# Attention and expert layers in one kernel: the first expert's first rows gathered after five batches instead of six, and the sixth batch's scatters spaced like those of the first five

## The chip, the cores and the metric

The kernel runs on one core of one Trainium2 chip. The metric is the device time of one execution in microseconds (us); less is better. The core has five engines that run side by side, each with its own queue of instructions, worked off in order: TensorE (PE, matmuls; PEld are its weight loads), VectorE (DVE), ScalarE (ACT), GpSimd (POOL) and SyncE (SP, which here only issues transfers). Transfers are issued from SP, ACT and POOL and run on 16 shared DMA engines.

## The reference

Causal attention with a decay, and then a layer of eight experts of which each token uses one:

```python
# q, k, v: 8 batches x 8 heads x 576 x 64; f: 8 x 8 x 576
cum = np.cumsum(np.log(np.clip(f, 0.0001, 1.0)), axis=-1)
scores = scale * q @ k.T + cum[..., :, None] - cum[..., None, :]     # above the diagonal: -1e9
attn = exp(scores - max) ; attn /= attn.sum(-1) + 1e-09
x = (attn @ v) as 4608 tokens x 512
logits = x @ w_gate ; e_idx = argmax(logits) ; gate_w = softmax(logits)[e_idx]
eom = sigmoid(x @ w_output_gate)
for e in range(8):                      # every token belongs to one expert
    h = maximum(x[e_idx == e] @ w1[e], 0)          # 512 -> 1024
    out[e_idx == e] = gate_w * eom[:, e] * (h @ w2[e])   # 1024 -> 512
```

With the inputs of the reference's default seed expert 0 gets 582 of the 4608 tokens: 434 of the first 3456 (six batches), and 360 of the first 2816, which is what five routed batches hold here (why not 2880 is told below).

## The kernel before, in words

**Two phases.** Attention and routing are one loop of steps (`attention`, L738), written out by hand: `now[0]` is the step, 192 of them do scores, and every piece of work is placed by an offset of the table `OFF` and, inside a step, by `OFF["order"]`. Each engine gets its instructions in just this order. Six steps make one pair of heads (u = 0 to 31), 24 steps one batch. Then come the experts, expert 0 first.

**Attention in a step.** PE makes a bank of scores (`sc`, L273), ACT takes the exponential (`p`, L381), POOL subtracts the upper half of each number from it (`plo`, L383; from step 181 on every second one is DVE's), and PE multiplies `p` and `plo` with V (`av`, L455 to L457 and L466 to L468). For the first head of a pair, the third bank's `plo` is made in step 6u+4 and read by PE in step 6u+6. Before a pair's scores SP writes the row maxima into the tile `Eq` (`max_put`, L361 and L363, at step 6u-5), and the scores of step 6u-1 read them. DVE normalizes (L488 to L495), POOL also splits V (`Vs`, L145).

**From attention to the experts.** When half of a batch's heads (u of 16) is done, `feats` casts the rows to pairs of 16-bit numbers (ACT L527, L145), five or four transposing transfers on SP make `xT` for the router (`feats_turn`, L534), and `feats_out` writes the rows to `xbuf` in DRAM (L541). A batch has 4 tiles of 128 tokens and 64 more. The last 64 of an even batch share a tile with those of the odd batch after it: they are written (two L546, one for each batch) and routed with the odd batch. So the first five batches (0 to 4) hold 4 x 576 + 512 = 2816 routed tokens, and the last 64 rows of batch 4 are written when batch 5 is, its second half at step 163.

**Routing.** `route` (L558) makes logits on PE (`lg`, L566, L567), ranks the tokens of the batch within each expert on DVE and PE, and then POOL scatters each tile's tokens into the table `tbl` (L650, one transfer to a tile), whose first rows are those of expert 0. `apart` says how many POOL operations lie between two scatters; the first scatter comes 13 steps after the route begins. For batch 5 neither held before: it scattered as soon as its ranks were there, with one operation between. `lg` and `rk` of the router, the small transposes and `hold` take turns in one PSUM bank (`tag="ms"`).

**The early rows.** The first three tiles (384 rows) of expert 0 are fixed before attention ends. `hold_early` (L548) counts expert 0's rows so far; where there are fewer than 384, it moves later rows of expert 0 behind row 384 and leaves the slots between empty. `early_gather` (L720) waits for the last scatter, reads the table's first 384 entries (`ids`, L701), gathers the rows on POOL into `xg` (L705, three transfers) and transposes them on SP (L711, three). Each gather reads `xbuf[0:known]`, where `known` is `EARLY_B * S`, and so it waits for every write into that part of `xbuf`.

**After attention.** PE does expert 0's up products on the three early tiles (`hp`, L934). Behind the sixth of eight groups of them stand the logits of batch 7, the last. Its scatters, then `ids` (L701), gathers and transposes lead to the rest of expert 0 and to expert 1. SP's queue holds the transposes for the logits of batch 7 behind all that stands before them. `CAP` is 640: an expert with more rows (expert 0's empty slots counted) would need another pass at the end.

Of the kernel before, what the change touches and what calls it, by code (L numbers as in the profile page):

```python
# [21 lines left out]
B, H, S, D = 8, 8, 576, 64  # L22
# [21 lines left out]
NSLOT = P  # L44
WSC = 64.0

EARLY_B = 6
ET = 3
EARLY = ET * P

# [2 lines left out]
OFF = {  # L53
    "crow": -12, "clear": -16, "clearstep": 1, "prefill": -11, "fetch": -23, "spread": -21, "max": -15, "pair": -8,
    "mturn": -7, "rows": -6, "put": -5, "rscore": 2, "rexp": 3, "av": 5, "fetch_v": (-19, -25, -21), "v": ((-2, -9, -16), (1, -7, -15)), "apart": 2, "scatter": 13,
    "feats0": 19, "feats1": 20, "fturn": 21, "fturnstep": 2, "fout": 31, "route": 45, "rank": 6, "w1r": 10, "w1": 48, "w1step": 2, "w2": 4,
    "hold": 188, "gather": 180, "ids": 5, "landed": 1, "gturn": 2, "route_last": 200, "nsum": 8, "nrec": 9, "nx": 9, "nrest": 10,
    "mv": ["xr", "v0", "v1"], "begin": -18, "wg": -4, "spread/1": -11,
    "steps": [0, 0, 0, 0, 0, 1, 8, 1], "dve": [181, 183, 185, 187, 189, 191],
    "order": "reduce put feats1 v0 scores nrec max pair rows spread feats0 fetch "  # L60
             "fetch_v fturn extra tick mturn tick v1 nx rexp av rscore maxrest route fout tick exps nsum tick nrest",
# [11 lines left out]
def _attn_moe(ctx, tc, qk, vm, f, wg, w1, w2, out):  # L73
# [67 lines left out]
    pooled = [0]  # L141
# [39 lines left out]
    apart = cp.tile([1, 1], F32, name="apart")  # L181
# [325 lines left out]
    last = 3 * HU * NU  # L507
# [48 lines left out]
    now = [0]  # L556

    def route(b, t0=None):  # L558
# [79 lines left out]
        for t in range(nt):  # L638
            at, n = now[0], pooled[0]
            yield  # L640

            while t0 is not None and b < EARLY_B - 1 and now[0] < t0 + OFF["scatter"]:
                yield

            while t0 is not None and now[0] < last and (now[0] == at or pooled[0] < n + (OFF["apart"] if t and b < EARLY_B - 1 else 1)):
                yield
            if b == B - 1 and t:

                nc.gpsimd.memset(apart, 0.0)
            ins = nc.gpsimd.indirect_dma_start(  # L650
                out=tbl, out_offset=bass.IndirectOffsetOnAxis(ap=pi[:, t:t + 1], axis=0),
                in_=rec[:, b, t], in_offset=None)

            for other in scatters:
                tc.declare_no_dep(ins.ins, other.ins, reason="distinct rows")
            scatters.append(ins)
# [47 lines left out]
    def gather_rows(x, t, known=NT):  # L704
        nc.gpsimd.indirect_dma_start(  # L705
            out=xg[:, t], out_offset=None, in_=xbuf[0:known],
            in_offset=bass.IndirectOffsetOnAxis(ap=x[0][:, t, 0:1], axis=0),
            bounds_check=known - 1, oob_is_err=False)
# [11 lines left out]
    def early_gather():  # L720
        while len(routed) < EARLY_B:
            yield

        at = now[0]
        while now[0] < at + OFF["landed"]:
            yield
        x = st["early"] = gather_ids(ar, tbl[0:EARLY], ET)
        at = now[0]
        for t in range(ET):
            while now[0] < at + OFF["ids"] + t:  # L730
                yield
            gather_rows(x, t, EARLY_B * S)
        for t in range(ET):
            while now[0] < at + OFF["ids"] + OFF["gturn"] + t:
                yield
            gather_turn(x, t)

    def attention():  # L738
# [12 lines left out]
        for s in range(OFF["begin"], last + OFF["nrest"] + 1):  # L751
# [80 lines left out]
            def extras():  # L832
                for f, fc in extra.get(s, ()):
                    f(fc)
                if s == OFF["hold"]:
                    assert routed == list(range(EARLY_B))
                    hold_early()
# [251 lines left out]
```

## Time and profile before

| | us |
|---|---|
| three runs | 832.22, 838.12, 838.7 |
| median | 838.12 |
| profiled execution, whole | 837.48 |
| its span, first to last instruction | 835.8 |
| attention, to the last `rk` matmul | about 387 |

The profile is one execution. A row of the timeline gives start and duration in us, engine, line, operation, output and input, how many were merged, and in brackets how long the engine had been idle before and what ended it. A row of the list of waits gives the total, how often, and the longest. A row of the windows gives the window and its length, the busy time and count of PE, PEld, DVE, ACT and POOL, then the granted TensorE clock (1.00 is 2.4 GHz, 0.50 is 1.2 GHz), the DMA engines' share and GB/s.

### The profile page before, as it was taken

To read this page: it belongs to the slowest core of one execution; us is meant where nothing else is said; L and a number is where in the kernel's file an instruction comes from. 1 tells how busy PE (TensorE), PEld (TensorE's weight loads), DVE (VectorE), ACT (ScalarE), POOL (GpSimd) and SP (SyncE) were. 2 spreads that over 40 slices of the span, in tenths; PEclk is the share of its full clock that TensorE was granted. 3 is DMA by queue.
4 is the path that set the end of the run, shared out by engine and by line. 5 is a ranking of instruction groups with operands and counts; after the bars stand their busy time and mean duration, and the time that the engine had idled before them with its cause. 6 is when DMAs were issued, how large, how long until landed. Compare 5 with 4: busy or idle time off the path is not lost. (4 is left out here: it accounts for less than half of the span.)

```text
span 835.8 us, 21243 instructions
## 1 busy us (share of the span) xinstructions
PE 765.8 (92%) x8814; PEld 499.7 (60%) x8814; DVE 348.6 (42%) x770; ACT 344.8 (41%) x767; POOL 475.1 (57%) x504
## 2 busy tenths in 40 slices
PE   1699999899999999977939999999999999999997
PEld 0377776667776676755516565656656566565653
DVE  4456676675868575735412511203112031120310
ACT  6055565465655564534302423415234153331420
POOL 9088778688887788865252523625437254361301
PEclk9999999999999999979978999999999999999999
DMA  3333758866697668327749554655645556444201
GB/s 102 127 122 79 183 146 178 167 151 143 151 186 154 105 156 117 96 65 126 128 105 280 194 97 144 180 128 170 161 131 160 131 166 167 124 140 101 73 14 43
DMA packets 132920, 112.61 MB, mean 135 GB/s; under 512 B 96024, under 2 KB 105426, under 8 KB 132820
## 3 DMA queue, kind: packets, MB, share of 16 engines
q1 hardware_dynamic: 121092, 75.19, 40.7%
q0 software_dynamic: 7552, 18.92, 7.4%
q10 hardware_dynamic: 4176, 17.11, 7.2%
q8 instruction: 70, 1.15, 0.6%
q14 instruction: 30, 0.25, 0.1%
HBM read 72.79 MB, written 20.48 MB: 112 GB/s over the span
## 5 line engine op out<-in xcount | busy, mean ns | idle before, releaser
L383 POOL TENSOR_TENSOR plo<-p 128x512 f16<-128x512 f32 x186 | 197.9, 1079 | 71.3 <-ACT p L381 69.4
L934 PE MATMUL hp<-xT,w1h 128*128 128x384 f16 (+1 forms) x1024 | 197.2, 303 | 19.8 <-DMA xT<-xg 18.2
L299 DVE TENSOR_REDUCE nR<-mx 128x2 f32<-128x1024 f32 (+4 forms) x160 | 126.6, 808 | 90.0 <-PE mx L273 77.8
L381 ACT ACTIVATE p<-sc 128x512 f32<-128x512 f32 x192 | 112.9, 595 | 80.0 <-PE sc L273 70.0
L934 PEld LDWEIGHTS <-w1h 128*128 128x128 f16 x1024 | 101.1, 99 | 66.2 <-DMA xT<-xg 14.4
L273 PE MATMUL sc<-qk 64*128 64x512 f32 (+4 forms) x640 | 137.2, 488 | 0.0
L934 PE MATMUL hp<-xT,w1l 128*128 128x384 f16 (+1 forms) x512 | 129.9, 303 | 0.0
L967 POOL DMA_INDIRECT out_dram<-ys,ids x40 | 41.8, 1046 | 151.5 <-ACT ys L966 103.3
L944 DVE SCALAR_TENSOR_TENSOR hl<-hp,hh 128x256 f16<-128x256 f32 (+1 forms) x128 | 60.5, 491 | 155.6 <-ACT hh L943 143.8
L963 PE MATMUL y<-w2l,hh 128*128 128x512 bf16 x320 | 120.5, 379 | 0.0
L962 PE MATMUL y<-w2h,hh 128*128 128x512 f16 x320 | 120.3, 379 | 0.0
L964 PE MATMUL y<-w2h,hl 128*128 128x512 f16 x320 | 119.3, 379 | 0.0
L273 PEld LDWEIGHTS <-pick 64*128 64x128 bf16 (+1 forms) x1152 | 64.0, 99 | 47.6 <-issue 25.1
L896 DVE TENSOR_TENSOR w2l<-w2r,w2h 128x512 bf16<-128x512 f32 x28 | 26.9, 961 | 148.7 <-ACT w2h L895 148.7
L966 ACT ACTIVATE ys<-y,ids 128x512 f32<-128x512 f32 x40 | 27.5, 687 | 134.6 <-PE y L964 95.2
L455 PE MATMUL av<-Vs,p 128*128 128x65 f16 x640 | 70.6, 195 | 10.0 <-ACT xr L502 6.4
L273 PE MATMUL mx<-qk 64*128 64x256 bf16 (+5 forms) x384 | 64.8, 312 | 14.8 <-DVE nR L299 8.8
L671 POOL TENSOR_TENSOR w1l<-w1r,w1h 128x512 bf16<-128x512 f32 x48 | 54.8, 1160 | 38.3 <-ACT w1h L670 38.2
L943 ACT ACTIVATE hh<-hp 128x256 f16<-128x256 f32 (+1 forms) x128 | 50.6, 433 | 58.6 <-PE hp L934 52.1
L670 ACT CAST w1h<-w1r 128x512 f16<-128x512 f32 x64 | 39.1, 617 | 85.6 <-issue 46.3
L457 PE MATMUL av<-Vs,plo 128*128 128x65 f16 x640 | 69.8, 193 | 4.8 <-POOL plo L383 4.6
L456 PE MATMUL av<-Vs,p 128*128 128x64 bf16 x640 | 70.1, 196 | 0.0
(156 smaller groups left out, 1424.6 us busy)
## 6 DMA issues: line engine op xcount, KB each, us to landing
qk<-in_qk_dram ACTq DMA_DIRECT2D x29, 576.0 KB
w1r<-in_w_dram SPq DMA_DIRECT2D x64, 256.0 KB
w2r<-in_w_dram SPq DMA_DIRECT2D x64, 256.0 KB
v<-in_vm_dram SPq DMA_DIRECT2D x16, 576.0 KB
xbuf<-x SPq DMA_DIRECT2D x16, 512.0 KB
qk<-in_qk_dram SPq DMA_DIRECT2D x3, 576.0 KB
xT<-x SPq DMA_TRANSPOSE x72
Eq<-mts SPq DMA_DIRECT2D x64, 0.1 KB
```

What stands on the lines that cost most here:

```text
L273: nc.tensor.matmul(dst(i), w(i), x(i), start=start, stop=stop)
L299: nc.vector.tensor_reduce(o, x, axis=AX.X, op=ALU.max, negate=True)
L381: nc.scalar.activation(out=f32, in_=src, func=AF.Exp, scale=0.125)
L383: eng.tensor_tensor(lo, f32, upper(f32), op=ALU.subtract)
L455: nc.tensor.matmul(dst, ph, vv[:, 0:W], start=kc == 0, stop=False)
L456: nc.tensor.matmul(dst[:, 0:D], ph, vv[:, W:].bitcast(BF16), start=False, stop=False)
L457: nc.tensor.matmul(dst, pl, vv[:, 0:W], start=False, stop=kc == qc)
L934: nc.tensor.matmul(m[:, 0:(t1 - t0) * P], w[:, k], xT[:, t0:t1, k // 2, j, k % 2], start=k == 0 and i == 0, stop=k == ND - 1 and i == 2)
L944: nc.vector.scalar_tensor_tensor(hl[:, fc, sl], m, 0.0, hh[:, fc, sl], op0=ALU.max, op1=ALU.subtract)
L962: nc.tensor.matmul(y, hh[:, fc, sl], wh, start=fc == 0, stop=False)
L963: nc.tensor.matmul(y, hh[:, fc, sl], wl, start=False, stop=False)
L964: nc.tensor.matmul(y, hl[:, fc, sl], wh, start=False, stop=fc == NF - 1)
```

## The change

The early rows come from five batches, the offsets of `hold` and `gather` move from steps 188 and 180 to 167 and 156, and the spacing rule of the scatters holds for batches 0 to 5, where it held for 0 to 4.

```diff
-EARLY_B = 6
+EARLY_B = 5
...
-    "hold": 188, "gather": 180, "ids": 5, "landed": 1, "gturn": 2, "route_last": 200, "nsum": 8, "nrec": 9, "nx": 9, "nrest": 10,
+    "hold": 167, "gather": 156, "ids": 5, "landed": 1, "gturn": 2, "route_last": 200, "nsum": 8, "nrec": 9, "nx": 9, "nrest": 10,
...
-            while t0 is not None and b < EARLY_B - 1 and now[0] < t0 + OFF["scatter"]:
+            while t0 is not None and b < B - 2 and now[0] < t0 + OFF["scatter"]:
                 yield

-            while t0 is not None and now[0] < last and (now[0] == at or pooled[0] < n + (OFF["apart"] if t and b < EARLY_B - 1 else 1)):
+            while t0 is not None and now[0] < last and (now[0] == at or pooled[0] < n + (OFF["apart"] if t and b < B - 2 else 1)):
                 yield
```

**POOL, the early gathers.** Before, they stood at steps 186 to 188, close to the end of attention:

```order
L383 TENSOR_TENSOR plo<-p_8219 128x512
L383 TENSOR_TENSOR plo<-p_8179 128x512
L705 DMA xg<-xbuf,ids 128x1024
L383 TENSOR_TENSOR plo<-p_8360 128x512
L705 DMA xg<-xbuf,ids 128x1024 x2
L397 TENSOR_TENSOR prl_97<-prf_96 128x128
```

Now they stand at steps 165 to 167, among the splits of V:

```order
L383 TENSOR_TENSOR plo<-p_7402 128x512
L705 DMA xg<-xbuf,ids 128x1024
L397 TENSOR_TENSOR prl_97<-prf_96 128x128
L383 TENSOR_TENSOR plo<-p_7456 128x512
L145 TENSOR_TENSOR Vs_93<-v_6851,Vs_93 128x9x64
L705 DMA xg<-xbuf,ids 128x1024
L383 TENSOR_TENSOR plo<-p_7402 128x512
L705 DMA xg<-xbuf,ids 128x1024
L383 TENSOR_TENSOR plo<-p_7456 128x512
```

The `plo` ahead of the third gather is that of step 166. Three gathers have moved ahead of some thirty POOL operations, and two of them now stand ahead of this `plo`. Batch 5's scatters, which stood one operation apart at steps 174 to 178, now begin at step 178 and stand two or three apart, the last at step 189.

**SP around the early gathers, as it is now** (`Eq` is the maxima's tile, `Ek` the decay's, `xT<-xg` the early rows' transposes, the other `xT` the router's):

```order
L701 DMA ids<-tbl 128x3x2
L534 DMA_TRANSPOSE xT_6937<-x_6938 128x4x128
L361 DMA Eq_87<-mts 2x4x128
L363 DMA Eq_87<-mts 1x16x4 x2
L541 DMA xbuf<-x_6938 128x4x512
L546 DMA xbuf<-x_6938 64x512 x2
L256 DMA Ek_80<-crow 6x576
L534 DMA_TRANSPOSE xT_7432<-x_7433 128x4x128 x2
L711 DMA_TRANSPOSE xT<-xg 128x8x128 x2
L361 DMA Eq_88<-mts 2x4x128
L363 DMA Eq_88<-mts 1x16x4 x2
```

`ids` and the three `xT<-xg` are what is new here. The first L546 writes the last 64 rows of batch 4, which the gathers read; it is issued at step 163, and the first gather stands at step 165.

**SP at the end of attention**, before:

```order
L711 DMA_TRANSPOSE xT<-xg 128x8x128
L534 DMA_TRANSPOSE xT_8378<-x_8379 128x4x128
L711 DMA_TRANSPOSE xT<-xg 128x8x128 x2
L534 DMA_TRANSPOSE xT_8378<-x_8379 128x4x128 x4
L541 DMA xbuf<-x_8379 128x4x512
L546 DMA xbuf<-x_8379 64x512 x2
L534 DMA_TRANSPOSE xT_8711<-x_8712 128x4x128 x5
```

And now:

```order
L534 DMA_TRANSPOSE xT_8391<-x_8392 128x4x128 x5
L541 DMA xbuf<-x_8392 128x4x512
L546 DMA xbuf<-x_8392 64x512 x2
L534 DMA_TRANSPOSE xT_8711<-x_8712 128x4x128 x5
```

The early rows' transposes no longer stand among those of batch 7, on which its logits wait.

## Rows read from the trace of the kernel before

**Rows 1.** The page: busy us of each engine, share of the span, instructions.

```profile
PE 765.8 (92%) x8814; PEld 499.7 (60%) x8814; DVE 348.6 (42%) x770; ACT 344.8 (41%) x767; POOL 475.1 (57%) x504
```

**Rows 2.** The list of waits, 340 to 470 us: total, times, longest.

```profile
PE hp L934 <- DMA xT<-xg: 18.2, 2, 14.1
...
PE av L457 <- POOL plo L383: 4.6, 1, 4.6
```

**Rows 3.** The timeline of PE: matmuls before which it had been idle.

```profile
363.95 0.23 PE L457 MATMUL av<-Vs,plo 128*128 128x65 f16 x1 [4.61 <-POOL plo L383]
379.54 0.33 PE L273 MATMUL rs<-qk 64*64 64x64 f32 x4 [0.65 <-DVE x L145]
391.42 0.80 PE L934 MATMUL hp<-xT,w1h 128*128 128x384 f16 x2 [4.11 <-DMA xT<-xg]
439.96 0.61 PE L934 MATMUL hp<-xT,w1h 128*128 128x256 f16 x2 [14.13 <-DMA xT<-xg]
```

**Rows 4.** Windows in which the granted clock went back up.

```profile
372.00:374.00 2.00, 2.00 (x44) 1.91 (x40) 0.00 (x0) 1.50 (x3) 0.90 (x1) 0.58 0.04 8
394.00:396.00 2.00, 2.00 (x13) 1.16 (x12) 0.52 (x1) 0.49 (x1) 0.46 (x1) 0.96 0.83 187
445.00:450.00 5.00, 5.00 (x46) 4.41 (x44) 1.52 (x4) 1.54 (x4) 0.95 (x1) 0.96 1.10 211
```

**Rows 5.** The timeline of POOL at steps 165 to 167.

```profile
334.77 0.40 POOL L397 TENSOR_TENSOR prl<-prf 128x128 f16<-128x128 f32 x1
...
336.13 1.25 POOL L145 TENSOR_TENSOR Vs<-v,Vs 128x576 bf16<-128x576 f32 x1
337.34 2.04 POOL L383 TENSOR_TENSOR plo<-p 128x512 f16<-128x512 f32 x2
```

**Rows 6.** The timeline of POOL: scatters, the late `plo`, and a gather.

```profile
324.20 0.99 POOL L650 DMA_INDIRECT tbl<-rec,pi  x1 [0.17 <-issue]
...
361.56 1.25 POOL L650 DMA_INDIRECT tbl<-rec,pi  x1 [0.17 <-issue]
362.84 3.03 POOL L383 TENSOR_TENSOR plo<-p 128x512 f16<-128x512 f32 x3
...
374.30 1.36 POOL L705 DMA_INDIRECT xg<-xbuf,ids  x1 [0.15 <-issue]
```

**Rows 7.** The timeline of PE: a wait for maxima, step 167's `av`, step 173's scores.

```profile
328.18 0.39 PE L273 MATMUL sc<-Eq,Ek 64*128 64x512 f16 x2 [1.46 <-DMA Eq<-mts]
...
340.05 0.20 PE L455 MATMUL av<-Vs,p 128*128 128x65 f16 x1
...
347.90 1.13 PE L273 MATMUL sc<-qk 64*128 64x512 f32 x4
```

**Rows 8.** The timeline of SP's queue at steps 157 to 169.

```profile
319.22 0.61 SPq L361 DMA_DIRECT2D Eq<-mts  x1
...
335.73 1.54 SPq L546 DMA_DIRECT2D xbuf<-x  x2
...
341.76 0.60 SPq L361 DMA_DIRECT2D Eq<-mts  x1
```

**Rows 9.** The timeline of SP's queue: `ids` and the first early transpose.

```profile
367.24 0.40 SPq L701 DMA_DIRECT2D ids<-tbl  x1
...
378.12 1.24 SPq L711 DMA_TRANSPOSE xT<-xg  x1
```

**Rows 10.** The window in which the transfers of step 163 end.

```profile
338.00:339.00 1.00, 1.00 (x8) 0.43 (x8) 0.93 (x3) 0.00 (x0) 1.00 (x2) 1.00 0.34 96
```

**Rows 11.** The timeline of SP's queue after attention.

```profile
385.15 3.44 SPq L711 DMA_TRANSPOSE xT<-xg  x2
...
396.23 8.43 SPq L534 DMA_TRANSPOSE xT<-x  x5
```

**Rows 12.** The last cast of batch 7 on DVE, and its logits on PE.

```profile
391.00 0.42 DVE L145 TENSOR_TENSOR x<-xr,x 128x256 f16<-128x256 f32 x1
...
405.49 0.19 PE L566 MATMUL lg<-wgs,xT 128*128 128x32 f16 x1 [0.16 <-DMA xT<-x]
```

## The prediction

> **What bounds the kernel now.** I read the page first, then the waits around the change, then the timeline of each engine there. TensorE is busy 92% of the span [rows 1], so a gain can only come from the few places where it stands still or runs at half clock. In the list of waits from 340 to 470 us two names matter: `plo` of POOL, 4.6 us once, and the early and later rows' transposes, 18.2 us in two waits [rows 2]. The timeline gives the places [rows 3]: PE stands 4.61 us until 363.95 (so from 359.34) for a `plo` that POOL makes behind batch 5's crowded scatters [rows 6]; 4.11 us until 391.42, between attention and the first `hp`, for the early rows; and 14.13 us until 439.96 for the rest of the rows, after a long chain that starts with batch 7's logits.
>
> After each of these waits the granted clock is 0.50 for a while. It returns in the windows of [rows 4]; a window at 0.58 of 2 us was full for 0.32 us, so after the first wait it returned at 373.7, 9.7 us after PE had started again. By the same reading it took 2.7 us after the second wait and 5.4 us after the third. Half clock costs half of that time where PE sets the pace: 4.9, 1.4 and 2.7 us.
>
> **The change part by part.**
>
> *Batch 5's scatters.* They were five in a row with one operation between, and the last `plo` behind them came at 362.84 to 363.9 [rows 6]. Now only one stands ahead of that `plo` (step 178). What this wait cost is 4.61 + 4.9 = 9.5 us. That goes, if POOL comes to step 178 in time. The other four scatters lie where the gathers were, about 1.4 us each against 1.5 us each; nothing there changes.
>
> *The gathers.* Three operations of 0.15 + 1.36 = 1.5 us [rows 6] move ahead to steps 165 to 167, where POOL starts its `prl` at 334.77 [rows 5]. Their place isn't empty, and the first one has a new wait. It reads `xbuf` up to row 2880, and the last 64 rows of that are written by the first L546, which SP issues at 335.73 [rows 8], after POOL has come to the gather. Those transfers end in the window from 338 to 339, a third of the way in by its DMA share [rows 10]: 338.4. SP is also a little later than before, since `ids` now stands ahead and waits for batch 4's last scatter. That one ends at 325.2, and a last scatter that ended at 362.8 let `ids` go at 367.24, 4.4 us later [rows 6, 9]: `ids` goes at 329.6 and costs the queue between nothing and 2 us; I take 0.7. So the first gather starts at about 339.1, and POOL, which works in order, does nothing from 334.8 until then. Then come gather 1.5, `prl` 0.4, `plo` 1.0, V's split 1.25, gather 1.5 and step 166's `plo` 1.0 [rows 5, 6]: 345.8. PE reads it right after the nine matmuls of step 167 that begin at 340.05 [rows 7], at about 340.35. **A new idle time of 5.4 us takes the place of the old one.** It is as long as those after which the clock fell; half clock then costs 1.4 to 4.9 us, and between the three rows I take the middle one, 2.7, since the nearest in place (4.9) had POOL behind as well. In sum 8.1 us (6.8 to 10.3) instead of 9.5: a gain of 1.4 (2.7 to -0.8).
>
> The Trainium skill's page "TensorE: Matmul & The Clock Gate", section "HAM oscillation — how this bites in real kernels", speaks against the change here: a long wait inside a stream of matmuls lets the gate fall, and the work after it starts slow, each time anew. By that the moved idle pays for the clock again, as in the sum; were the clock to stay, the sum would be 830 (POOL would then set the pace at step 178). All three waits of over 4 us in this trace agree with the page.
>
> *Does the old wait come back?* From 345.8 to step 178's `plo` POOL has one gather, twelve `plo`, three splits of V, two `prl`, one scatter and a small product: 1.5 + 12.2 + 3.75 + 0.8 + 1.4 + 0.3 = 20 us, so 365.8. PE, 8.1 us late, wants it at 367.5, and at 366.1 in the mildest case. So no second stall, by little.
>
> *`hold`.* Its matmul and three small DVE operations are the same. They share a PSUM bank with the small transposes, and the matmul behind waited 0.65 us [rows 3]; at step 167 that falls into the new idle time: a gain of 0.65.
>
> *`ids` and the transposes on SP.* The three L711 leave the end of attention. There two of them held SP's queue for 3.44 us [rows 11], ahead of nine of batch 7's ten transposes. Batch 7's last cast ended at 391.4 [rows 12], yet its last five transposes began at 396.23 [rows 11], and the logits waited for them at 405.49 [rows 12]. So the queue, not the data, was late, and the logits come 3.4 us earlier after attention's end (0 if the transfers themselves set the pace, 5.5 if all of what PE gains counted). From the logits to 439.96 the chain is the same work, so the end moves by that much.
>
> *The wait at 391.42* goes whole, with its half clock: 4.11 + 1.4 = 5.5 us of PE time. Counted at 3.4 only, already above: PE comes earlier to batch 7's logits, and now waits there about 2 us for SP. The 14.13 us wait stays.
>
> *The data.* With 360 early rows, 24 slots stay empty; 582 + 24 = 606 is under 640, so no pass is added. The gathers move the same three tiles.
>
> **The sum.** 1.4 + 0.65 + 3.4 = 5.4 us off the profiled execution's 837.5: **832 us**. That execution is 0.6 us under the median of 838.1. This case's own range is 829 to 836: the half clock gives 1.3 down and 2.2 up, the queue at the end 2 us each way.
>
> The Trainium skill's "DMA: Bandwidth & Descriptors", section "Anatomy of one DMA — SWDGE (gpsimd) path", gives a transfer issued by POOL about 2.0 us in all before its bytes count. By it `ids` would go over 3 us sooner, the 0.7 us would be nothing, and the sum 831.4. The trace shows 5.7 us from the scatter's start to `ids` [rows 6, 9], and that decides.
>
> **The rivals.**
>
> *The gathers hold nothing up.* If the 64 rows have landed when POOL gets there, step 166's `plo` ends at 341.5 and PE waits 1.1 us, step 178's at 361.4 and PE waits 0.9 more: 2.0 instead of 9.5 us. With 3.4 at the end that is 10.9 off: **826.6**. For it: POOL may come later than in this trace. Against it: 335.73 is after 334.77 without any delay, and SP only gets more to do.
>
> *The transposes on SP hold up the maxima: slower than before.* Two L711 stand ahead of the put for the scores of step 173. The second waits for the second gather, which ends at 344.8; a gather that ended at 375.66 let its transpose go at 378.12 [rows 6, 9], 2.5 us later, or 4.4 as after the scatter. So the put, at 341.76 before [rows 8], goes at 348.5 to 350.5. The scores stood at 347.90 [rows 7] and are 8.1 us late, 356.0. This decides from about 7 us of landing on: a put begun at 319.22 kept PE until 328.18 [rows 7, 8], 9 us, with the queues full. Then PE waits another 2.5 us or so and the clock falls again (1.4 to 4.9): up to 7.4 us more, **839 to 840**. Twice in a row, for the next pair as well, would be 847. Against it: 328.18 is the only such wait I found late in attention.
>
> *The end doesn't move.* If batch 7's transposes run at the pace of the DMA engines (the last five took 8.43 us [rows 11]), nothing is won there, and it is **835.5**. Against it: 4.8 us between the last cast and the first of the five.
>
> **How the numbers follow.** Forecast 0.52, gathers free 0.18, SP slower 0.12, end unmoved 0.18. The range that leaves out no more than 2 in 10 is 825 to 840: it takes in the forecast's own range, the third rival and most of the first two. Within 1% (8.4 us, about what a measurement of this kernel can tell from no change, as its three runs span 6.5) means 829.7 to 846.5. Faster: most of the first rival and the forecast's low end, 0.27. Slower: the second rival doubled, 0.06. Same: 0.67.
>
> **What would show it.** Right: POOL stands some 4 us before its first gather; PE stands about 5 us near 340 on `plo`, with clock 0.50 after it; none near 360; `hp` follows `rk` without a gap; the last five `xT` transposes begin within 2 us of the last cast; the 14 us wait is still there. Wrong: a wait on `Eq` near 356, a late `plo` near 366, or logits that come no sooner after the last cast. Above 840 or under 825 a step that I have not seen is at work.

## The result, and the profile after

| | before | changed |
|---|---|---|
| median of 11 runs each, us | 837.36 | 842.31 |
| lowest to highest | 832.22 to 841.7 | 838.72 to 846.0 |
| profiled execution, its span | 837.48, 835.8 | 845.94, 844.2 |

The ratio is 1.0059, 95% interval 1.0034 to 1.0084: slower by 5 us, where 5.4 us less were forecast. A repeat on another chip, where the kernel before took 829.56, gave 1.0039 (1.0019 to 1.0059). The ratios leave out executions over 1.5% above the fastest of their kernel, which the medians keep: one of six in e9 and five of twelve in e10, whose medians alone give 0.993 and 0.991, and one each in e12 and e15. The profile shown in this section is 3.6 us above the median of its kernel.

The list of waits of PE, 300 to 470 us, answers to [rows 2]: total, times, longest.

```profile
PE hp L934 <- DMA xT<-xg: 15.5, 1, 15.5
PE lg L566 <- DMA xT<-x: 10.1, 3, 5.2
PE av L457 <- POOL plo L383: 4.4, 1, 4.4
```

The `hp` wait for the early rows is gone. A `plo` wait is there, but at a new place. A wait that was not in the sum has come in: the router's logits (`lg`) wait for their transposes. PE's timeline gives the places, as in [rows 3].

```profile
342.94 0.21 PE L566 MATMUL lg<-wgs,xT 128*128 128x32 f16 x1 [4.41 <-DMA xT<-x]
...
353.45 0.23 PE L457 MATMUL av<-Vs,plo 128*128 128x65 f16 x1 [4.41 <-POOL plo L383]
...
393.87 0.48 PE L934 MATMUL hp<-xT,w1h 128*128 128x384 f16 x2
...
411.85 0.21 PE L566 MATMUL lg<-wgs,xT 128*128 128x32 f16 x1 [5.16 <-DMA xT<-x]
...
450.12 0.61 PE L934 MATMUL hp<-xT,w1h 128*128 128x256 f16 x2 [15.51 <-DMA xT<-xg]
```

Two waits of 4.41 us stand in the middle of attention: batch 5's logits, and ten us later the `plo` behind the gathers. None is near 360, and `hp` follows without a gap. The windows (the granted clock is the third number from the end) show a granted clock of 0.62 to 0.70 around and behind both.

```profile
340.00:345.00 5.00, 2.06 (x23) 1.46 (x25) 0.92 (x4) 0.00 (x0) 0.00 (x0) 0.67 0.64 101
345.00:350.00 5.00, 3.79 (x45) 2.06 (x41) 2.12 (x3) 1.66 (x3) 2.54 (x4) 0.65 0.57 138
350.00:355.00 5.00, 1.55 (x15) 1.24 (x17) 3.67 (x11) 0.31 (x1) 4.62 (x5) 0.70 0.56 143
355.00:360.00 5.00, 5.00 (x68) 3.48 (x66) 0.93 (x3) 1.97 (x7) 5.00 (x6) 0.62 0.46 102
```

SP's queue shows where it starts, first its list of waits and then its timeline, as in [rows 8, 9].

```profile
SPq L701 <- DMA tbl<-rec,pi: 8.5, 1, 8.5
```

```profile
337.96 0.40 SPq L701 DMA_DIRECT2D ids<-tbl  x1
338.83 1.24 SPq L534 DMA_TRANSPOSE xT<-x  x1
...
343.61 1.47 SPq L546 DMA_DIRECT2D xbuf<-x  x2
```

`ids` stood 8.5 us at the head of the queue. Behind it stood the last transpose for batch 5's logits, which is PE's first wait, and the 64-row write, on which the first gather waits. POOL's timeline, as in [rows 5, 6], has the other end.

```profile
325.85 0.99 POOL L650 DMA_INDIRECT tbl<-rec,pi  x1 [0.17 <-issue]
...
347.44 1.06 POOL L705 DMA_INDIRECT xg<-xbuf,ids  x1 [12.40 <-DMA Ek<-crow]
...
352.35 1.05 POOL L383 TENSOR_TENSOR plo<-p 128x512 f16<-128x512 f32 x1
```

Batch 4's last scatter starts at 325.85, and what reads it goes 12.1 us later. POOL then stands 12.40 us ahead of the first gather. (The row names the transfer that came last by the profile; by the program the gather waits for `ids` and the 64 rows.)

**Where the 8.4 us between the two profiles are.** Three points cut the span: the start of batch 4's last scatter (324.20 and 325.85), the last `rk` of attention (batch 6's), the last `lg` of batch 7, and the late `hp` at 439.96 and 450.12. The first stretch is cut once more: PE's idle time (gaps of over 0.15 us), and what half clock took, which is (1 - granted clock) times PE's busy time, summed over windows of 2 us.

| profile | scatter to last rk | idle | clock | rest | rk to last lg | lg to late hp |
|---|---|---|---|---|---|---|
| before | 62.9 | 7.4 | 4.8 | 50.7 | 18.9 | 33.9 |
| changed | 68.0 | 10.2 | 5.2 | 52.5 | 19.1 | 37.2 |

1.65 us of the 8.4 lie ahead of the change, 5.1 in the first stretch, 0.2 and 3.2 in the other two, and behind the late `hp` 1.8 come back.

### The profile page after: what moved, and what is told of

Read it like the earlier page. It is cut to its first block, busy times and chain, and to the rows that moved or that the text cites. A ratio compares the mean times of both kernels' runs of the same rounds, so it can differ in the third digit from the quotient of the medians.

```text
span 844.2 us, 21239 instructions
## 1 busy us (share of the span) xinstructions
PE 768.9 (91%) x8814; PEld 500.7 (59%) x8814; DVE 349.4 (41%) x770; ACT 344.7 (41%) x767; POOL 473.9 (56%) x504
## 5 line engine op out<-in xcount | busy, mean ns | idle before, releaser
L896 DVE TENSOR_TENSOR w2l<-w2r,w2h 128x512 bf16<-128x512 f32 x28 | 25.1, 896 | 149.7 <-ACT w2h L895 149.7
L273 PE MATMUL mx<-qk 64*128 64x256 bf16 (+5 forms) x384 | 65.3, 315 | 13.9 <-DVE nR L299 8.3
```

Of the source, the lines that this page charges most:

```text
L273: nc.tensor.matmul(dst(i), w(i), x(i), start=start, stop=stop)
```

## The experiments

Theory 1 when they began: `ids` waits for batch 4's last scatter at the head of SP's queue, and makes the logits and the 64-row write late; PE pays for both, and for the clock. Theory 2: only the gather's wait for the 64 rows. Theory 3: the gathers' own load on POOL. The experiments ran in four sessions on chips on which the kernel before took 828.01 (e1 to e4), 829.56 (e5 to e8), 836.89 (e9 to e12) and 829.16 us (e13 to e16), so each is read as a ratio to the kernel before on its chip.

**e1, ids late.**

```diff
-    "hold": 167, "gather": 156, "ids": 5, "landed": 1, "gturn": 2,
+    "hold": 167, "gather": 156, "ids": 5, "landed": 7, "gturn": 2,
```

> One number changed against the changed kernel: ids is read seven steps after batch 4's last scatter instead of one, so at step 166, behind batch 5's last logits transpose and the 64-row write on SP's queue; the gathers move with it to steps 171 to 173, their transposes to 173 to 175. Theory 1 (ids, waiting for the scatter's 11 us landing at the head of SP's queue, makes both the logits of batch 5 and the 64 rows late): the lg wait near 343 (4.4 us) and the plo wait near 353 (4.4 us) both go, SP waits under 1 us on ids, the first gather runs without an idle POOL ahead of it, and the time falls by 9 to 14 us against the changed kernel: 829 to 833. Theory 2 (only the gather's wait for the 64 rows): the plo wait goes and the lg wait stays: 5 to 7 us less, 835 to 837. Theory 3 (the load of three gathers on POOL itself, 4.5 us in a busy stretch): a plo wait of 3 to 5 us turns up near 365 to 375 instead, and the time is as in the changed kernel, 839 to 843.

829.87 us, ratio 1.0020 (0.9997 to 1.0042). The `plo` wait fell to 0.2 us, batch 5's logits did not wait, and POOL was not idle ahead of its gather, as theory 1 had it. But by the two ratios only about half of the slowdown went (the changed kernel has 1.0039 in e5, and the two intervals overlap), not the 9 to 14 us expected. PE had new waits, for the maxima of DVE (`nR`):

```profile
356.27 0.40 PE L273 MATMUL mx<-qk 64*128 64x256 bf16 x2 [2.92 <-DVE nR L299]
```

**e2, known.**

```diff
-            gather_rows(x, t, EARLY_B * S)
+            gather_rows(x, t, EARLY_B * S - EARLY_B % 2 * SR)
```

> One bound changed against the changed kernel: the early gathers read xbuf only up to row 2816, which holds every row that five routed batches can name, so they no longer wait for the 64-row write of step 163. ids stays at step 160 and still waits for the scatter. Theory 1: the lg wait (4.4 us, with its half clock) stays as it is, SP still stands about 8 us at ids; the first gather goes at about 340.5 instead of 347.4, as soon as ids has landed, and the plo wait near 353 goes or shrinks under 1.5 us: 4 to 7 us less than the changed kernel, 835 to 838. Theory 2 (only the 64 rows): both waits go, 829 to 832. Theory 3 (POOL's load): the plo wait stays at 3 us or more, 840 to 843.

827.31 us, ratio 0.9992 (0.9972 to 1.0012). The first gather went 12.0 us behind the scatter (318.13 to 330.13), not 21.6, and PE waited 1.07 us for `plo`. The interval lies wholly under that of the changed kernel (1.0019 to 1.0059), so the wait for the 64 rows is most of its loss. All the same it is no faster than before, and here the trace shows why: PE, DVE and POOL, a timeline of each.

```profile
351.61 0.29 PE L273 MATMUL mx<-qk 64*128 64x256 bf16 x2 [3.30 <-DVE nR L299]
```

```profile
343.79 5.70 DVE L620 TENSOR_TENSOR tmp<-tmp,oh 128x40 f32<-128x40 f32 x1
...
350.27 1.28 DVE L299 TENSOR_REDUCE nR<-mx 128x2 f32<-128x768 f32 x2
```

```profile
342.50 1.24 POOL L145 TENSOR_TENSOR Vs<-v,Vs 128x576 bf16<-128x576 f32 x1
343.70 0.39 POOL L397 TENSOR_TENSOR prl<-prf 128x128 f16<-128x128 f32 x1
344.06 2.03 POOL L383 TENSOR_TENSOR plo<-p 128x512 f16<-128x512 f32 x2
346.06 0.19 POOL L627 TENSOR_TENSOR sc<-sc 128x5 f32<-128x5 f32 x1
346.21 1.22 POOL L145 TENSOR_TENSOR Vs<-v,Vs 128x576 bf16<-128x576 f32 x1
347.40 2.03 POOL L383 TENSOR_TENSOR plo<-p 128x512 f16<-128x512 f32 x2
```

L620 works on 128x40 numbers and took 0.20 us in the kernel before (at 348.01). Here it stands 5.70 us, from 343.79 to 349.49, and POOL's unbroken row of operations ends at 349.43. The reduction that PE waits for stands behind it in DVE's queue. In e1 L637 took 2.83 us in place of 0.16, until 355.01, and POOL's row ended at 355.00. I call this theory 1b: the moved gathers take POOL's pauses, and a DVE operation with two operands in SBUF stands until POOL pauses. It is theory 3 in another form: the load is paid on DVE, not on `plo`. Two limits belong to it. Not every such operation stood until the end of the row: in e1 L594 stood 1.10 us until 339.37, when one of POOL's operations ended (339.31) and the next followed at once. And in the changed kernel's own two profiles L620, the cast L629 and L637 took 0.16 to 0.20 us; only `hold`'s L554 stood there, 2.98 us in the first profile, while PE waited for `plo` anyway.

The Trainium skill's page "SBUF — State Buffer", section "Who interferes with whom", has it that VectorE and GpSimd share a port pair, which one of them holds for a whole instruction, and that a VectorE instruction with two SBUF inputs, or a copy or cast in a fast mode, competes for it. The traces agree; that the loser can stand over a row of POOL instructions, seven in the trace of e2, is what they add.

**e3, batch 5 as tight as before.**

```diff
-            while t0 is not None and b < B - 2 and now[0] < t0 + OFF["scatter"]:
+            while t0 is not None and b < B - 3 and now[0] < t0 + OFF["scatter"]:
...
-... (OFF["apart"] if t and b < B - 2 else 1)):
+... (OFF["apart"] if t and b < B - 3 else 1)):
```

> The changed kernel with the old spacing for batch 5 alone: its scatters stand one POOL operation apart again and begin as soon as its ranks are there; the early rows still come from five batches at steps 165 to 167. All theories have the two waits near 343 and 353 stay as in the changed kernel. If the spacing was worth the 9.5 us that I counted (4.6 us of waiting near 360 and 4.9 us of half clock), this is 7 to 10 us slower than the changed kernel: 849 to 852. If PE, being late by 10 us or more from the two new waits, has already given POOL the time that it lacked, no wait shows near 360 to 375 and it is within 2 us of the changed kernel.

836.87 us, ratio 1.0112 (1.0094 to 1.0131), and the changed kernel has 1.0039 in e5: the spacing is worth about 0.7%, 6 us, a little under the 7 to 10 expected. PE's timeline has both waits, the one of the gathers and the old one, the latter as long as in [rows 3]:

```profile
342.63 0.23 PE L457 MATMUL av<-Vs,plo 128*128 128x65 f16 x1 [7.85 <-POOL plo L383]
...
368.57 0.20 PE L457 MATMUL av<-Vs,plo 128*128 128x65 f16 x1 [4.61 <-POOL plo L383]
```

**e4, the read alone in the kernel before.**

```diff
+            if s == 160:
+                nc.sync.dma_start(ar.tile([P, CT, 2], I32, name="ids")[:, 0:ET],
+                                  tbl[0:EARLY].rearrange("(t p) c -> p t c", p=P))
```

> The kernel before with one transfer more: at step 160 SP also reads the table's first 384 entries, into a buffer that nothing uses; gathers, hold and spacing are those of the kernel before. It is the read of ids alone at its new place. Theory 1: SP stands 7 to 10 us at this read until about 338, batch 5's last logits transpose behind it is late, and PE waits 4 to 5 us for lg near 343; PE and POOL have then a new relation, so the wait for plo near 360 (4.6 us) may shrink: the time is 836 to 844, and the profile decides. Theory 2 and 3 (the read itself is harmless): the read waits under 2 us, no lg wait over 1 us, time within 1.5 us of the kernel before.

828.84 us, ratio 1.0013 (0.9990 to 1.0036), no `lg` wait, and 2.3 us of waiting at the read, for a transpose. It went at 326.92, 8.5 us behind its scatter (318.40). Against theory 1: the read alone does PE no harm in this trace. (In the first profile, where it went 12.1 us behind, it did, through the logits.)

**e5, the changed kernel once more,** without an edit.

> The changed kernel itself, not edited, once more: the chip of the first four experiments ran the kernel before in 828.0 us, the chip of the first comparison in 837.4, so the changed kernel needs a time beside theirs. Theory 1: ids waits 7 to 12 us for batch 4's last scatter at the head of SP's queue, the 64-row write goes behind it, PE loses 8 us or more before 360 in one or two waits (lg, plo) and 4 to 6 us to the half clock after them, and logits of batch 7 come no sooner after the end of attention: 1.004 to 1.008 of the kernel before. If the slowdown belongs to that one chip: 0.994 to 1.001.

831.55 us, ratio 1.0039 (1.0019 to 1.0059). Its profile is the fastest of its runs, 825.91, so it shows a mild case. It has one wait in place of two. PE, SP and POOL:

```profile
342.50 0.24 PE L457 MATMUL av<-Vs,plo 128*128 128x65 f16 x1 [7.31 <-POOL plo L383]
```

```profile
325.67 0.40 SPq L701 DMA_DIRECT2D ids<-tbl  x1
...
331.56 1.99 SPq L546 DMA_DIRECT2D xbuf<-x  x2
```

```profile
336.49 1.06 POOL L705 DMA_INDIRECT xg<-xbuf,ids  x1 [7.67 <-DMA xbuf<-x]
```

`ids` goes 6.9 us behind the scatter (318.77), the logits do not wait, and yet the gather comes at 336.49, 17.7 us behind the scatter, since the write is issued 12.8 us behind it and the gather follows another 4.9 later. Of the changed kernel's two profiles the `lg` wait belongs to the first alone, the wait for the 64 rows to both. Even in this mild case the loss in attention is there: idle 9.5 and clock 3.1 us, 64.4 in the table's first stretch.

**e6, known and ids late.** The edits of e1 and e2 together.

```diff
-    "landed": 1,
+    "landed": 7,
...
-            gather_rows(x, t, EARLY_B * S)
+            gather_rows(x, t, EARLY_B * S - EARLY_B % 2 * SR)
```

> Two edits against the changed kernel: the gathers read xbuf only up to row 2816 (no wait for the 64-row write), and ids is read seven steps after batch 4's last scatter (gathers at steps 171 to 173). Theory 1: each edit alone takes the two waits away, and together they give nothing more than one: within 2 us of the kernel with ids late alone; the wait for nR of DVE near 356 (2.9 us there) stays, since it comes from the ranks of batch 5 on DVE and not from the gathers. Theory 2: as theory 1. Theory 3 (POOL's load): also the same. If the two add up, it is 3 us or more below either.

832.02 us, ratio 1.0039 (1.0017 to 1.0061). The gathers now hold up nothing (`plo` 0.38 us), and L637 stands 2.84 us, with 3.77 us of waiting for `nR` behind it. Nothing is won over the changed kernel (1.0039 too): one wait has taken the other's place.

**e7, the last write behind the transposes.**

```diff
-                fturn=turns, fout=lambda: each("fout", NQ - 1, 12, feats_out),
+                fturn=turns, fout=lambda: each("fout", NQ - 2, 12, feats_out),
...
+        feats_out(NQ - 2)
```

> One thing moved against the changed kernel: the last feats_out that stands between the two groups of five transposes for batch 7's logits (one L541 of 512 rows and two L546 of 64 rows, written to xbuf) goes behind both groups. If these writes hold up the last transposes, the logits of batch 7 end 4 to 5 us sooner after attention (14 to 15 us behind the last rk instead of 19), the wait of 15.5 us for the later rows starts as much earlier, and the time is 3 to 5 us under the changed kernel on the same chip. If the transposes run at the DMA engines' own pace, or the tables and gathers behind them then wait for the writes instead, nothing moves: within 1.5 us.

827.31 us, ratio 1.0000 (0.9974 to 1.0027), 4 us under the changed kernel. From the last `rk` to the last `lg` it is 13.8 us, 15.6 in e5: the write between the two groups of five transposes had held up the second. The two profiles are equally long (825.99 and 825.91), so of the 4 us they show only these 1.7.

**e8, all three:** the edits of e1, e2 and e7, whose added lines are these.

```diff
-    "landed": 1,
+    "landed": 7,
...
+            gather_rows(x, t, EARLY_B * S - EARLY_B % 2 * SR)
...
+        feats_out(NQ - 2)
```

> The three edits together: gathers read up to row 2816, ids seven steps after the scatter, and the last feats_out behind batch 7's last transposes. Theory 1 has no wait of over 3 us in attention, hp behind rk without a gap, and at the end what the last feats_out alone brings: 8 to 12 us under the changed kernel, 3 to 7 us under the kernel before (0.992 to 0.996). If the writes at the end are not what is late: as the kernel with the first two edits.

829.07 us, ratio 0.9994 (0.9966 to 1.0023). L637 stood 2.84 us again, and in a profile 3.2 us above the median idle and clock in attention came to 8.3 and 6.5. Theory 1 alone had missed this.

**e9, known and ranks in PSUM.** The edit of e2, and:

```diff
-        nc.vector.tensor_tensor(tmp, rkv, eoff[:, 0:nt], op=ALU.add)
+        nc.vector.tensor_tensor(rkv, rkv, eoff[:, 0:nt], op=ALU.add)
...
-        nc.vector.tensor_tensor(tmp, tmp, oh, op=ALU.mult)
+        nc.vector.tensor_tensor(tmp, rkv, oh, op=ALU.mult)
...
-        so = ar.tile([P, E], BF16, name="so")
+        so = rk[:, NTB * E:NTB * E + E]
```

> The kernel whose gathers read up to row 2816 (known), and in the router three operands moved from SBUF to PSUM: the ranks' sum is written back into the bank of rk, and the small counts go there too, so that the two DVE operations of batch 5's ranks (L620, L637) read one operand from SBUF instead of two. With known alone, L620 stood 5.70 us from 343.79 to 349.49, until the last of POOL's unbroken run of operations had ended (349.43), and PE waited 3.30 us for nR behind it and lost 3.1 us to half clock. Theory 1b (a DVE operation with two operands in SBUF stands while POOL works without a pause, and the moved gathers have taken POOL's pauses): L620 and L637 take 0.2 us each wherever POOL is, the wait for nR near 34 us after batch 4's last scatter goes, and the time is 2 to 6 us under known alone, 0.992 to 0.997 of the kernel before. Rival (DVE is late for another reason, or the long row is an artefact of the trace): the wait for nR stays at 2.5 us or more, ratio 0.998 to 1.002.

831.35 us, ratio 0.9889 (0.9833 to 0.9945). In the profile L620 takes 0.20 us, and the next operation with its operands in SBUF stands in its place, a cast; DVE and POOL:

```profile
349.14 0.20 DVE L620 TENSOR_TENSOR tmp<-rk,oh 128x40 f32<-128x40 f32 x1
...
349.64 5.18 DVE L629 CAST pi<-sc 128x5 int32<-128x5 f32 x1
...
355.05 0.16 DVE L637 TENSOR_TENSOR runs<-runs,rk 128x8 bf16<-128x8 bf16 x1
```

```profile
352.76 2.03 POOL L383 TENSOR_TENSOR plo<-p 128x512 f16<-128x512 f32 x2
```

It stands until 354.82; POOL's row ends at 354.79. The wait for `nR` went, one of 4.28 us for L637 took its place (the bank of `rk` is now held until then). This profile (834.85) is 3.5 us above the median and shows no gain over e2's in the first stretch (65.3 against 63.1 us); the gain of e9 rests on its times alone.

**e10, the same with the last write moved,** the edits of e9 and e7:

```diff
+        nc.vector.tensor_tensor(tmp, rkv, oh, op=ALU.mult)
...
+        feats_out(NQ - 2)
```

> As the one before, and the last feats_out behind batch 7's last transposes. Theory 1b and the end together: logits of batch 7 end 13.8 to 14.1 us behind the last rk, no wait of over 2 us in the last 60 us of attention: 0.990 to 0.995 of the kernel before, under both kernels. If something else becomes late in attention again, 0.997 or more.

829.43 us, ratio 0.9859 (0.9818 to 0.9900). Here POOL pauses between 349.43 and 349.85, and the cast, at 349.69, takes 0.17 us. The last `lg` comes 15.1 us behind `rk`, later than the 13.8 to 14.1 expected.

**e11, gathers behind the ranks,** with the edit of e7 and

```diff
-    "landed": 1,
+    "landed": 10,
```

> The changed kernel with ids ten steps behind batch 4's last scatter, so that the gathers stand at steps 174 to 176, behind batch 5's ranks and ahead of its first scatter (step 178), and with the last feats_out moved as before. Theory 1b: POOL keeps its pauses while batch 5's ranks are made, L620 and L637 take 0.2 us, no wait for nR near 34 us after the scatter; instead POOL has three gathers and the first scatter in five steps, 4.5 us more than it has room for, so plo is late by 1 to 4 us near step 178: 0.995 to 1.000. If the wait for nR is there as before (2.5 us or more), theory 1b falls.

835.36 us, ratio 0.9987 (0.9955 to 1.0018). L620, L629 and L637 did not stand, and `plo` was 1.85 us late near step 178, both as expected of theory 1b. DVE's casts of the rows and one `plo` of its own stood (1.95 to 2.93 us); in the kernel before one of each did too (1.98 and 2.19).

**e12, the last write moved in the kernel before.**

```diff
-                fturn=turns, fout=lambda: each("fout", NQ - 1, 12, feats_out),
+                fturn=turns, fout=lambda: each("fout", NQ - 2, 12, feats_out),
...
+        feats_out(NQ - 2)
```

> The kernel before, with the last feats_out behind batch 7's last transposes and nothing else. In the kernel before SP reaches those transposes 3 us later, because of the early rows' transposes ahead of them, so the writes are hidden less or more: if the logits of batch 7 end 1.5 to 2 us sooner after the last rk than 18.6 to 18.9, as they do in the changed kernel, the time is 1 to 2 us under the kernel before (0.997 to 0.999); if SP's queue alone sets them there, 1.000.

834.73 us, ratio 0.9966 (0.9929 to 1.0003): not told apart from no change, and the last `lg` came 18.3 us behind `rk`, hardly sooner.

**e13, the changed kernel with ranks in PSUM,** now the positions too: the edits of e9 without that of e2, and

```diff
+        pos = rk[:, NTB * E + E:NTB * E + E + nt]
         nc.vector.tensor_reduce(pos, tmp, axis=AX.X, op=ALU.add)
```

> The changed kernel with the router's ranks made through PSUM: the sum of L616 stays in the bank of rk, and the positions (L623) and counts (L635) go there too, so that L620, the cast L629 and L637 have at most one operand in SBUF or none of the size that stood. Gathers, ids and writes are as in the changed kernel. Theory 1 (ids on SP's queue, then the gather's wait for the 64 rows): POOL stands 7 to 12 us ahead of its first gather as before, PE waits 7 us or more in one or two places near 15 to 28 us behind batch 4's last scatter, so PE is late and POOL has pauses when batch 5's ranks come: nothing to win, 1.002 to 1.007 of the kernel before, as the changed kernel. If the moved gathers cost by the lock alone, it is 0.990 to 0.997.

826.24 us, ratio 0.9969 (0.9948 to 0.9990). PE waits 8.31 us for the `plo` behind the gathers, as theory 1 said, but the time is under its range of 1.002 to 1.007, since ranks in PSUM gain in the kernel before as well (e14). The gain over the changed kernel (0.7%) is about what they gain there.

**e14, the kernel before with ranks in PSUM,** the edit of e13:

```diff
+        pos = rk[:, NTB * E + E:NTB * E + E + nt]
```

> The kernel before with the same ranks through PSUM and nothing else. In its trace L620, L629 and L637 of batch 5 took 0.16 to 0.20 us each, so theory 1b gives it nothing there: 0.997 to 1.002. If the ranks of other batches stood behind POOL too, or PSUM is better in itself, it is under 0.994, and the gain of the kernels with ranks in PSUM is not that of the changed place of the gathers.

824.01 us, ratio 0.9942 (0.9917 to 0.9966). This I had not expected. In the kernel before, L620 took 0.81 us in batches 0 to 3 and L637 about 1 us in two of them; here 0.20 and 0.16. There they did not stand until the end of POOL's row: L637 of batch 1 stood until 175.34, one POOL operation ended at 175.31, and the next followed at once. PE's wait behind batch 1's ranks shows the gain, in the profile of before and here:

```profile
179.59 0.19 PE L455 MATMUL av<-Vs,p 128*128 128x65 f16 x1 [1.66 <-DVE x L145]
```

```profile
175.91 0.19 PE L455 MATMUL av<-Vs,p 128*128 128x65 f16 x1 [0.66 <-DVE x L145]
```

Batch 3's ranks have the same (1.67 and 0.67 us). Behind these two waits PE also lost time to half clock. The first window is from the profile of before, behind batch 3's ranks, the second from e14, at the same place:

```profile
268.00:270.00 2.00, 2.00 (x20) 1.25 (x17) 1.61 (x4) 1.22 (x4) 1.85 (x4) 0.50 1.00 331
```

```profile
262.00:264.00 2.00, 2.00 (x32) 1.45 (x30) 1.86 (x5) 1.27 (x5) 1.85 (x4) 1.00 0.96 353
```

In eleven of the twelve traces with ranks in SBUF the granted clock fell to 0.50 behind the ranks of batch 1, batch 3 or both, and cost 1.7 us each time; in none of the six with ranks in PSUM did it fall there. Two new waits of 0.7 us, for L638, stand behind the ranks of batches 0 and 2. Two waits of 1 us less and 1.7 to 3.4 of half clock, less 1.4 for the new waits, are 2.3 to 4.0 of the 5 us (an estimate).

**e15, known, the last write moved and ranks in PSUM:** the edits of e2, e7 and e13.

```diff
+            gather_rows(x, t, EARLY_B * S - EARLY_B % 2 * SR)
...
+        pos = rk[:, NTB * E + E:NTB * E + E + nt]
...
+        feats_out(NQ - 2)
```

> The changed kernel with gathers that read up to row 2816, the last feats_out behind batch 7's last transposes, and ranks with positions and counts through PSUM. Before, with positions still in SBUF, the cast L629 stood 5.18 us behind POOL in one trace and 0.17 in another, and the time was 0.986 of the kernel before. Theory 1b: L620, L629 and L637 take 0.2 us in any case, idle time of PE from batch 4's last scatter to the last rk under 6 us: 0.982 to 0.990.

817.07 us, ratio 0.9850 (0.9815 to 0.9886): the best. The granted clock is 1.00 from the gathers to the end of attention, and PE loses 5.1 us to idle time and nothing to the clock. The windows, and PE's longest wait in them:

```profile
330.00:340.00 10.00, 8.08 (x146) 5.84 (x144) 8.54 (x21) 4.42 (x13) 9.62 (x10) 1.00 0.79 181
340.00:350.00 10.00, 8.83 (x177) 6.49 (x175) 6.90 (x20) 5.79 (x15) 9.62 (x11) 1.00 0.36 83
350.00:360.00 10.00, 10.00 (x201) 7.69 (x195) 4.28 (x12) 5.91 (x15) 8.91 (x11) 1.00 0.32 68
360.00:370.00 10.00, 9.91 (x197) 7.59 (x193) 7.04 (x13) 6.46 (x14) 7.33 (x8) 1.00 0.35 67
```

```profile
344.82 0.22 PE L348 MATMUL mt<-identh,mh 128*9 128x128 f16 x1 [1.17 <-DVE runs L638]
```

POOL is busy 9.62 of 10 us in the first two of them, without a pause from 334.25 to 347.43, and yet DVE's L620, its cast (here L630) and L637 (here L638) take 0.16 to 0.20 us inside that row. DVE and POOL:

```profile
341.79 0.20 DVE L620 TENSOR_TENSOR tmp<-rk,oh 128x40 f32<-128x40 f32 x1
...
342.30 0.16 DVE L630 CAST pi<-rk 128x5 int32<-128x5 f32 x1
...
344.60 0.16 DVE L638 TENSOR_TENSOR runs<-runs,rk 128x8 bf16<-128x8 bf16 x1
```

```profile
341.70 0.39 POOL L397 TENSOR_TENSOR prl<-prf 128x128 f16<-128x128 f32 x1
342.06 2.03 POOL L383 TENSOR_TENSOR plo<-p 128x512 f16<-128x512 f32 x2
344.05 0.19 POOL L628 TENSOR_TENSOR sc<-sc 128x5 f32<-128x5 f32 x1
344.20 1.24 POOL L145 TENSOR_TENSOR Vs<-v,Vs 128x576 bf16<-128x576 f32 x1
```

In the same trace two operations that still have both operands in SBUF stood, L585 for 1.71 and `hold`'s L554 for 1.72 us, each until POOL's row ended.

**e16, the same without the early rows from five batches:** the kernel before with the edits of e7 and e13.

```diff
+        pos = rk[:, NTB * E + E:NTB * E + E + nt]
...
+        feats_out(NQ - 2)
```

> The kernel before with the last feats_out behind batch 7's last transposes and the ranks through PSUM: what the two edits give without the early rows from five batches. With theory 1b the gathers at the end of attention leave POOL its pauses while batch 5's ranks are made, so only the writes' move counts: 0.995 to 0.999, as the kernel before with that move alone (0.9966). If it comes down to the kernel with all edits (0.982 to 0.990), the early rows from five batches bring nothing.

823.52 us, ratio 0.9941 (0.9915 to 0.9966), a little under the range expected and as e14: here too the last write's move wins nothing in the kernel before. Its interval and that of e15 do not touch: 6.5 us between the two medians is what the change is worth once its two costs are out. Between the two profiles the first stretch is 2.0 us shorter and the way from the last `rk` to the last `lg` 5.0.

The cut of the spans, as in the table above, for the kernels that decide:

| profile | scatter to last rk | idle | clock | rest | rk to last lg | lg to late hp |
|---|---|---|---|---|---|---|
| e4, before and a read | 61.5 | 8.3 | 1.5 | 51.7 | 18.6 | 33.8 |
| e5, changed | 64.4 | 9.5 | 3.1 | 51.9 | 15.6 | 32.5 |
| e2, known | 63.1 | 7.7 | 3.1 | 52.3 | 16.0 | 33.7 |
| e1, ids late | 66.5 | 7.6 | 6.1 | 52.8 | 15.6 | 34.9 |
| e13, changed, PSUM | 65.3 | 10.9 | 2.3 | 52.1 | 15.9 | 34.6 |
| e14, before, PSUM | 60.0 | 6.6 | 2.4 | 51.0 | 18.8 | 33.1 |
| e15, all | 57.9 | 5.1 | 0.0 | 52.8 | 13.8 | 33.2 |
| e16, e15 without the early rows | 59.9 | 6.4 | 2.6 | 50.9 | 18.8 | 32.6 |

## Why the prediction was wrong

**The step that failed** is "`ids` goes at 329.6 and costs the queue between nothing and 2 us; I take 0.7", together with 338.4 for the end of the 64-row write, and so "So the first gather starts at about 339.1". By it the gather starts 14.9 us behind batch 4's last scatter. In the five traces with `ids` and the gathers as changed (the first profile, e3, e5, e7 and e13) it started 17.7 to 21.6 us behind it, and PE's new wait (in the first profile two, 8.8 us in sum) was 7.3 to 8.8 us, not 5.4. Two terms were too small.

The first is `ids`. By the forecast it goes 5.4 us behind the scatter. It went 6.6 to 12.1 us behind it in the ten traces that have `ids` or the read next to it, at step 160 (12.1 in the first profile, 6.9 in e5). The one row that I took it from, of a scatter at 361.56, lies in a stretch with little traffic (a DMA share of 0.17 from 365 to 370), the new place in one with 0.55 to 0.73 (325 to 340); that this makes the difference was not tried by itself. The write behind it went 1.3 us later than before against the scatter in e5 and 6.2 in the first profile, where I had taken 0.7.

The second is the write itself. I read its end from a DMA share, 2.7 us behind its issue; from its issue to the gather it was 3.8 to 4.9 us in the five traces. In e5 this is the larger part: of the 2.8 us that the gather is late there, the write's issue makes up 0.6 and what follows it the rest. In the first profile it is 5.5 of 6.7.

In the first profile the new wait was two of 4.41 and 5.2 us of half clock, 14.0 us, in e5 one of 7.31 and 3.1, 10.4 (half clock over the whole stretch); the forecast had 8.1. e2, which takes the wait for the write away, brings the kernel back to the time of before: that shows it.

**The old wait** was priced at 9.5 us, 4.61 and 4.9 of half clock. The 4.6 us came again in every later trace with the old spacing (e3, e4, e12, e14, e16). The half clock did not: over the stretch it took 1.5 us in e4, 2.4 in e14, and 4.8 in the profile of before. I read one profile as the rule; the wait costs 6 to 9.5 us. That it goes is right (no wait near 360 in the changed kernel, and e3 lays it back).

**The logits behind `ids`** were left out: SP's queue holds batch 5's last transpose there. It cost 4.41 us in the first profile, nothing in e5, and 1.70 in e10.

**`hold`** was right in size (0.65 gone; 0.25 at its new place, where the gathers are late, and 0.83 and 0.85 in e2 and e15, where they are not). That its DVE operations are the same was wrong: L554 stood 1.72 to 2.98 us in e2, e15 and the first profile, 0.17 before and in e5. **The end**: 3.4 us sooner was forecast, 3.0 came in e5 (18.6 to 15.6), none in the first profile (18.9 to 19.1), where the last five transposes began at 400.45, 6.6 us behind the last `rk`, against 9.1 before, and PE yet waited 5.16 us for them. The rival "the end doesn't move" held there; e7 shows that the write in between is part of it.

**The rivals.** "The gathers hold nothing up" was made true by e2, whose PE waited 1.07 us for that `plo` where the rival had 1.1, and gave nothing like 826.6, 10.9 under the kernel before. So a second step failed, one that I never wrote: that nothing else is late when POOL loses 4.5 us of pauses. It was DVE's operations on the ranks, which stand while POOL works: the traces of e2 and e15 show it, and e15 against e16 what it is worth together with the wait for the write. In the changed kernel, where POOL is held up first, this second step costs little (L620, the cast and L637 took 0.16 to 0.20 us); it is why e2, with the first one out of the way, is no faster than the kernel before. "The transposes on SP hold up the maxima" did not come about.

The Trainium skill's page "DMA: Bandwidth & Descriptors", section "Anatomy of one DMA — SWDGE (gpsimd) path", which I had set against the trace, gives about 2.0 us in all. With 6.6 to 12.1 us the runs here lie further from it than from the 5.7 of my row.

**What stays open.** The changed kernel's two profiles lie 3.6 above and 5.6 us under their medians, so what its median run pays in each place is not shown. What decides between a stand of one POOL operation and one of a whole row is not shown. The 5 us that e14 wins are seen in part. The "rest" of the first stretch is about 1 us more in most kernels with early gathers (not in e3, 51.0); I did not look for it.

## What to carry to other kernels

Before a read is moved close behind what it waits for, ask how long that takes to land in the traffic of the new place, and who stands behind it in its queue: here the price of the wait was that of the write and the gather behind it. An engine's idle time can be what another engine lives on: DVE's short operations got through in POOL's pauses, and filling these turned 0.2 us into more than 5. A wait that comes again needs more than one profile before its half clock is priced: 4.6 us of waiting cost between 1.5 and 4.8 us more.

## What the runs showed of the hardware

A DVE operation on 128x40 numbers with both operands in SBUF took 0.20 us with POOL idle and 5.70 in a row of POOL operations, until that row ended (349.49 and 349.43); a cast on 128x5 5.18 (354.82 and 354.79). With an operand in PSUM the same work took 0.16 to 0.20 inside such a row (e15, 334.25 to 347.43). Other operations with both operands in SBUF got through when one POOL operation ended and the next followed (1.06 and 1.10 us). A scatter of 128 rows of 8 bytes let its reader go 6.6 to 12.1 us after its start at one and the same place of the program, and 5.7 at another.
